# A GpSimd scaling step issued three steps later in an attention pipeline

## The chip, the cores and the metric

The kernel runs on one core of one Trainium2 chip. The metric is device time in microseconds (us), from launch to end. The kernel before takes 1523.18 us, the median of three runs (1522.98 to 1523.98).

## The reference

Four layers stand one behind the other, each with a residual: a spectral filter, an attention, and the same two again with the same weights. The sequence has 2048 rows of 512 values in bfloat16.

```python
x = x + A(layernorm(x))      # A: rfft2, times (w_r + 1j*w_i), irfft2
x = x + B(layernorm(x))      # B: attention, 32 query heads of width 16, one key/value head
x = x + A(layernorm(x))
x = x + B(layernorm(x))

scores = einsum("bhqd,bkd->bhqk", q, k) * 16 ** -0.5
o = einsum("bhqk,bkd->bhqd", softmax(scores), v)
B = o.transpose(0, 2, 1, 3).reshape(1, 2048, 512) @ wo
```

Only the attention matters here. Its softmax is divided late: the kernel carries one extra column of ones beside v, which gives the sum of the weights, and each head's output is multiplied by the reciprocal of that sum.

## The kernel before, in words

Each of the two attention layers is cut into 32 **groups**, numbered from 0: four query blocks of 512 rows, and in each eight groups of four heads. A group has 64 score tiles of 128 keys by 512 queries, 16 key chunks for each of four heads. `run` (L560) writes out one order for all engines by hand. It goes in **steps**: 579 for a layer, 18 for a group (the first group has 20). A step n does this:

- `act_step` (L780): TensorE makes three or two score tiles in turn (`sc`, L681), and ScalarE takes the exponential of all of them in one instruction (`e`, L790).
- `dv_score` and `dv_pass` (L809, L819): TensorE makes one more score tile (`dv`, L681). VectorE turns it into a first image (`t_new`, L824), an integer whose bits, read as bfloat16, approximate the exponential. Nineteen tiles of a group (thirteen of the first) go this way, in batches of six, seven and six. The score banks for `dv` are two, used by turns. A projection (below) borrows one of them from the step that issues it to the next.
- `image_step` (L827): each batch needs three more images, which differ from the first by an added constant. VectorE makes two of them, each for the whole batch in one **image pass** (`s_new`, L839), at the first and the fourth of the batch's six steps. GpSimd makes the third, tile by tile (`pool_new`, L843), over the same six steps: two tiles in the first step of the seven-tile batch and one in each later one. `pace` (L685) makes each of these GpSimd instructions wait for the image pass issued last.
- `pv_step` (L792): TensorE multiplies images and exponentials, two or more steps old, with the values (`pv_new`, L803).

Counted from a group's first step, the seven-tile batch has steps 6 to 11 and the third batch steps 12 to 17. So the image passes of the seven-tile batch are issued in steps 6 and 9, and the third batch's in steps 12 and 15. This text calls them **pass 6, pass 9, pass 12 and pass 15**, after their steps.

When a group's sum is complete, in step 3 of the next group, `evict` (L696) lets VectorE transpose it out of PSUM (L706), one step later take the reciprocal of the sums (L707), and three steps later GpSimd multiply the values with it: `normalise` (L734). For query blocks 0 to 2 that is one instruction (L739) which writes into `block`. After a block's eighth group, `turned_block` (L726) has the SyncE queue turn the block with four DMA transposes (L732) for the output projection. In query block 3 the multiplication is L717, and after every second group VectorE transposes the result back (L723), again three steps later.

Two kinds of projection are placed among the steps. The next group's queries (L485) come in step 7 of every group, with a VectorE instruction each in the next two steps (L491, L495). The output projection of a finished block (L754) comes in step 13 of groups 9 to 12, 17 to 20 and 25 to 28, with the residual on VectorE (L759) a step later. In step 13 of these groups no `pv_new` is issued.

All instructions of an engine keep the order in which they are issued. The functions `later` and `later_pool` put a call into a step that lies so many steps ahead. In a step, the calls of `later` come before the images, and those of `later_pool` behind the images and before `pv_step`.

Of the kernel before, what the change touches and what calls it, by code (L numbers as in the profile page):

```python
# [18 lines left out]
NT, NC, R, T, NQB, HG = 16, 4, 4, 4, 4, 8  # L19
# [453 lines left out]
class Attention:  # L473
# [86 lines left out]
    def run(self, row_done, work, psums, final):  # L560
# [25 lines left out]
        NG = NQB * HG  # L586
# [35 lines left out]
        for n0 in range(NS):  # L622
            lst = []
            if n0 in d_phase:
                g, b, k, tiles = d_phase[n0]
# [29 lines left out]
        for n in range(NS + LAG + 2):  # L655
# [5 lines left out]
            g = evict_at.get(n + 1)  # L661
# [23 lines left out]
        def pace(ins):  # L685
            if image[0] is not None:
                tc.add_manual_dep(ins.ins, image[0].ins.name, mybir.DependencyInfo(
                    mybir.DependencyClass.Sync, mybir.DependencyReason.DATA), reason="pace")

        def later(steps, fn):  # L690
            todo.setdefault(now[0] + steps, []).append(fn)

        def later_pool(steps, fn):
            todo_pool.setdefault(now[0] + steps, []).append(fn)

        def evict(g):  # L696

            ps = pv.pop(g)
            o = small.tile([P, 16, 32], F32, tag="oraw")
            den = small.tile([P, 16], F32, tag="den")  # L700
            if g == NG - 1:
                for half in HALVES:
                    nc.vector.transpose(out=o[:, half, :].rearrange("p c j -> p (c j)"), in_=ps[:, 32 * half.start:32 * half.stop])
                ends.extend((o, den))
                return
            nc.vector.transpose(out=o.rearrange("p c j -> p (c j)"), in_=ps)  # L706
            later(1, lambda: nc.vector.reciprocal(out=den, in_=o[:, :, DH]))  # L707
            later_pool(3, lambda: normalise(g, o, den))

        ends = []  # L710

        def scaled_values(engine, g, o, den, c=slice(0, 16)):
            if g % 2 == 0:
                od_new = small.tile([P, 16, 32], BF, tag="od")
                turned_od[g // 2] = od_new
            half = slice(DH * (g % 2), DH * (g % 2) + DH)
            return engine.tensor_tensor(out=turned_od[g // 2][:, c, half], in0=o[:, c, 0:DH],  # L717
                                        in1=den[:, c].unsqueeze(2).broadcast_to([P, c.stop - c.start, DH]), op=ALU.mult)
# [3 lines left out]
        def turned_back(g, c=slice(0, 16)):  # L722
            nc.vector.transpose(out=otc[g // HG][:, g % HG // 2, 32 * c.start:32 * c.stop],  # L723
                                in_=turned_od[g // 2][:, c, :].rearrange("p c j -> p (c j)"))

        def turned_block(qb):  # L726

            turned = small.tile([P, 4, 512], BF, tag="be", bufs=1)
            otc[qb] = turned
            flat = od8[0].rearrange("p a b -> p (a b)")  # L730
            for h in range(4):
                nc.sync.dma_start(out=turned[:, h, :].rearrange("p (c q) -> p c q", c=16), in_=flat[32 * h:32 * h + 32, :], transpose=True)  # L732

        def normalise(g, o, den):  # L734
            if g < NG - HG:
                if g % HG == 0:
                    block = small.tile([P, 4, 512], BF, tag="bx", bufs=1)
                    od8[0] = block
                pace(nc.gpsimd.tensor_tensor(out=od8[0].rearrange("p a (c g d) -> p (a c) g d", c=4, g=HG)[:, :, g % HG, :], in0=o[:, :, 0:DH],  # L739
                                             in1=den.unsqueeze(2).broadcast_to([P, 16, DH]), op=ALU.mult))  # L740
                if g % HG == HG - 1:
                    turned_block(g // HG)
                return
            if g % HG == 0:
                ot_new = small.tile([P, 4, 512], BF, tag="otc", bufs=2)
                otc[g // HG] = ot_new
            pace(scaled_values(nc.gpsimd, g, o, den))
            if g % 2:
                later(3, lambda: turned_back(g))
# [115 lines left out]
        for n in range(NS + LAG + 2):  # L865
            now[0] = n
            act_step(n)
            dv = dv_score(n)
            for fn in pending:
                fn()  # L870
            del pending[:]
            if n in evict_at:
                evict(evict_at[n])
            dv_pass(n, dv)
            for fn in todo.pop(n, ()):
                fn()
            image_step(n)
            for fn in todo_pool.pop(n, ()):
                fn()
            pv_step(n)  # L880
            if n in piece_at:
                piece(*piece_at[n])
            for i, k in EARLY.get(NS - n, ()) if final else ():
                if k == 0:
                    ps = psd.tile([P, 512], F32, tag=f"dv{i}")
                    early.append(ps)
                last_project(i, early[i], (k,))
            chain()
# [260 lines left out]
```

## Time and profile before

| what | value |
|---|---|
| median of three runs | 1523.18 us |
| the profiled execution's own time | 1522.62 us |
| its span, first to last instruction | 1520.8 us |
| mean granted TensorE clock | 0.994 |
| busy: TensorE, VectorE, ScalarE, GpSimd | 88%, 93%, 94%, 51% |

The profile's page gives each engine's busy time and the costliest groups of instructions. The timeline view lists one engine's instructions in order of time: start in us, duration in us, engine, line, operation, what is written and read, its shape, and how many of one kind follow each other (x3). In square brackets stands the idle time before it and what ended that. Of several instructions in one row the duration covers them all, and records of one engine may overlap a little, since the next starts while the last one drains. The windows view adds up each engine's busy time in a stretch.

### The profile page before, as it was taken

The numbers are of one execution on the slowest core, as the hardware profiler recorded it, in microseconds if no ns is written. First come the engines' busy times: TensorE is split into PE (matmuls) and PEld (weight loads), VectorE is DVE, ScalarE is ACT, GpSimd is POOL, SyncE is SP. The second block draws the span as 40 slices with busy tenths as digits, with TensorE's granted clock in tenths as the row PEclk, the third lists the DMA queues.
The fourth block names the chain that finished last, engine by engine and source line by source line (L and its number), as shares of the span: only waits on it lengthen the run. The fifth ranks groups of instructions, "written<-read, shape, count | busy, mean of one in ns | idle before, by whom it ended". The sixth has DMA issues, their size and how long they took to land.

```text
span 1520.8 us, 33089 instructions
## 1 busy us (share of the span) xinstructions
PE 1337.1 (88%) x13186; PEld 427.5 (28%) x13186; DVE 1421.6 (93%) x2267; ACT 1427.3 (94%) x1349; POOL 780.1 (51%) x1310
## 2 busy tenths in 40 slices
PE   5988888899889988999899788889998899889987
PEld 2532222222222222222235222222222222222222
DVE  7888999999999999999989899999999999999996
ACT  4669999999999999999965899999999999999998
POOL 1005555555566555655600155555656555665555
PEclk9999999999999999999999899999999999999999
DMA  8120000100000000100010200000000000010000
GB/s 291 22 56 2 2 1 2 15 2 1 2 16 2 1 1 2 15 2 1 2 47 14 43 1 2 2 1 19 5 2 4 19 5 5 4 19 5 5 5 18
DMA packets 40655, 25.15 MB, mean 17 GB/s; under 512 B 31796, under 2 KB 37940, under 8 KB 40244
## 3 DMA queue, kind: packets, MB, share of 16 engines
q1 hardware_dynamic: 40116, 21.99, 5.8%
q8 instruction: 103, 1.69, 0.5%
q0 software_dynamic: 384, 1.05, 0.2%
q14 instruction: 52, 0.43, 0.1%
HBM read 14.64 MB, written 2.10 MB: 11 GB/s over the span
## 4 chain that ended last, share of the span: by engine, by line
ACT 51%; issue 22%; DVE 15%; PE 7%; POOL 1%; POOLq 0%; DVEq 0%; ACTq 0%
ACT e L790 49%; DVE t_new L824 7%; DVE s_new L839 4%; PE sc L681 1%; PE pv_new L803 1%; DVE st L161 1%; PE new L273 1%; PE new L443 1%; POOL pool_new L843 1%; DVE o L706 1%; PE new L311 0%; PE new L413 0%; DVE x_sb L459 0%; PE dv L681 0%; ACT X_new L188 0%
## 5 line engine op out<-in xcount | busy, mean ns | idle before, releaser
L790 ACT ACTIVATE e<-sc 128x1536 bf16<-128x1536 f32 (+1 forms) x1158 | 1312.7, 1300 | 4.2 <-PE dv L681 2.6
L843 POOL TENSOR_SCALAR pool_new<-t_new 128x512 int16<-128x512 int16 x1204 | 729.5, 629 | 701.9 <-DVE s_new L839 609.3
L824 DVE TENSOR_SCALAR t_new<-dv 128x512 uint16<-128x512 f32 x1204 | 790.1, 678 | 61.7 <-PE dv L681 54.3
L803 PE MATMUL pv_new<-e,vaug 128*32 128x512 bf16 x2892 | 583.3, 386 | 0.0
L681 PE MATMUL sc<-qt,KT 32*128 32x512 bf16 x2892 | 455.1, 384 | 123.4 <-ACT e L790 118.6
L681 PE MATMUL dv<-qt,KT 32*128 32x512 bf16 x1204 | 450.6, 384 | 18.9 <-DVE t_new L824 16.0
L803 PE MATMUL pv_new<-s_new,vaug 128*32 128x512 bf16 x2408 | 426.6, 385 | 1.9 <-DVE s_new L839 1.2
L839 DVE TENSOR_SCALAR s_new<-t_new 128x3584 int16<-128x3584 int16 (+1 forms) x380 | 403.3, 1062 | 0.1
L681 PEld LDWEIGHTS <-KT 32*128 32x128 bf16 x4096 | 157.9, 91 | 563.0 <-issue 559.7
L803 PE MATMUL pv_new<-pool_new,vaug 128*32 128x512 bf16 x1204 | 300.9, 384 | 1.4 <-POOL pool_new L843 1.4
L803 PEld LDWEIGHTS <-vaug 128*32 128x32 bf16 x7708 | 155.2, 94 | 370.4 <-issue 339.0
L803 PE MATMUL pv_new<-t_new,vaug 128*32 128x512 bf16 x1204 | 231.3, 385 | 0.1
L485 PE MATMUL ps<-xz,wq_sb 128*128 128x512 bf16 x248 | 65.2, 385 | 0.9 <-DVE t_new L824 0.8
L273 PE MATMUL new<-tab_F,xz 128*128 128x512 bf16 x192 | 46.5, 389 | 7.4 <-DVE xz L237 7.4
L491 DVE TENSOR_SCALAR qt<-ps,kq 128x512 bf16<-128x512 f32 x62 | 46.0, 742 | 1.2 <-PE ps L485 1.2
L706 DVE STREAM_TRANSPOSE o<-pv_new 128x512 f32<-128x512 f32 x62 | 43.7, 706 | 0.0
L188 ACT ACTIVATE X_new<-x_sb,ln_nb,ln_rstd 128x512 bf16<-128x512 bf16 x43 | 32.8, 804 | 8.0 <-DVE ln_nb L173 5.6
L161 DVE BATCH_NORM_STATS2 st<-x_sb 128x6 f32<-128x512 bf16 x52 | 33.5, 676 | 3.9 <-DMA x_sb<-in_A_x_dram 3.7
L168 ACT ACTIVATE ln_rstd<-ln_mv,ln_eps 128x4 f32<-128x4 f32 (+1 forms) x15 | 4.5, 297 | 30.8 <-DVE ln_mv L165 30.8
L485 PEld LDWEIGHTS <-wq_sb 128*128 128x128 bf16 x256 | 22.1, 97 | 32.2 <-issue 17.1
L739 POOL TENSOR_TENSOR block<-o,den 128x256 bf16<-128x256 f32 x48 | 29.9, 623 | 0.0
L197 ACT CAST x_new<-new 128x1024 bf16<-128x1024 f32 x14 | 14.2, 1012 | 16.4 <-PE new L311 15.1
(125 smaller groups left out, 586.0 us busy)
## 6 DMA issues: line engine op xcount, KB each, us to landing
tab_F<-const_F SPq DMA_DIRECT2D x5, 640.0 KB, 8.6
t_new<-const_IE SPq DMA_DIRECT2D x2, 1024.0 KB
x_sb<-in_A_x_dram SPq DMA_DIRECT2D x3, 512.0 KB, 7.0
rt<-in_A_w_r_dram SPq DMA_DIRECT2D x1, 1028.0 KB, 8.4
rt<-in_A_w_i_dram SPq DMA_DIRECT2D x1, 1028.0 KB, 6.6
t_new<-const_IO SPq DMA_DIRECT2D x2, 512.0 KB
woh<-in_B_wo_dram SPq DMA_DIRECT2D x16, 64.0 KB, 2.4
out_dram<-x_sb SPq DMA_DIRECT2D x8, 128.0 KB, 2.4
```

The lines of the kernel that those rows point to most:

```text
L161: self.nc.vector.bn_stats(st, x_t[:, r, :])
L188: engine.activation(out=xn_ap, in_=x_ap, func=ACT.Identity, bias=nb, scale=rs)
L273: self.mm(ps, lhsT=z, rhs=tab, start=start and i == 0, stop=stop and i == len(mms) - 1)
L485: self.nc.tensor.matmul(ps, lhsT=self.aw["wq"][:, c, hg, :], rhs=self.xT[:, 4 * qb:4 * qb + 4, c, :], start=(c == 0), stop=(c == NC - 1))
L491: self.nc.vector.tensor_scalar(out=qt, in0=ps, scalar1=self.kq[:, 1:2], scalar2=None, op0=ALU.mult)
L681: nc.tensor.matmul(dst, lhsT=KT[hs, kc * P:(kc + 1) * P], rhs=QT[g][hs, :], start=True, stop=True)
L706: nc.vector.transpose(out=o.rearrange("p c j -> p (c j)"), in_=ps)
L790: nc.scalar.activation(out=e[:, 0:na, :], in_=sc[:, 0:na, :], func=ACT.Exp, scale=SCALE)
L803: nc.tensor.matmul(pv[g][32 * h:32 * h + 32, :], lhsT=vaug[:, max(j, 0), kc, :], rhs=rhs, start=(first_pv[(g, h)] == u), stop=(last_pv[(g, ...
L824: nc.vector.tensor_scalar(out=tb[(g, b)][:, i, :], in0=dv, scalar1=T_MUL, scalar2=T_ADD, op0=ALU.mult, op1=ALU.add)
L839: image[0] = nc.vector.tensor_scalar(out=s_new[:, lo:nt, :], in0=src[:, lo:nt, :], scalar1=PH_OFF[i], scalar2=None, op0=ALU.add)
L843: pace(nc.gpsimd.tensor_scalar(out=sb[(g, b, 3)][:, i, :], in0=src[:, i, :], scalar1=1.0, scalar2=PH_OFF[3], op0=ALU.mult, op1=ALU.add))
```

## The change

One number in `evict` is replaced. For query blocks 0 to 2 (`g` below 24) the multiplication is issued six steps behind the eviction, and no longer three. Query block 3 keeps three.

```diff
             nc.vector.transpose(out=o.rearrange("p c j -> p (c j)"), in_=ps)
             later(1, lambda: nc.vector.reciprocal(out=den, in_=o[:, :, DH]))
-            later_pool(3, lambda: normalise(g, o, den))
+            later_pool(3 if g >= NG - HG else 6, lambda: normalise(g, o, den))
```

The eviction lies in step 3 of the next group. So the instruction L739 moves from step 6 to step 9 of groups 1 to 24 of each layer, 48 instances. On GpSimd's queue it stood behind the seven-tile batch's first two tiles and ahead of its third and fourth. It now stands behind the fifth tile, which is the first one after pass 9, and ahead of the sixth and seventh. Through `pace` it waits for pass 9 where it waited for pass 6. After groups 7, 15 and 23 the four DMA transposes move along with it. Nothing else changes: the number of instructions, their shapes and the work of the other engines stay.

## The prediction

> **What bounds the kernel now.** I began with the page's costliest groups, to see which engine is full and how much time each party to the change takes.
>
> ```profile
> L790 ACT ACTIVATE e<-sc 128x1536 bf16<-128x1536 f32 (+1 forms) x1158 | 1312.7, 1300 | 4.2 <-PE dv L681 2.6
> L843 POOL TENSOR_SCALAR pool_new<-t_new 128x512 int16<-128x512 int16 x1204 | 729.5, 629 | 701.9 <-DVE s_new L839 609.3
> L739 POOL TENSOR_TENSOR block<-o,den 128x256 bf16<-128x256 f32 x48 | 29.9, 623 | 0.0
> ```
>
> ScalarE's exponentials fill 1312.7 us and wait 4.2 us in all, so they set the end. The moved instruction lasts 0.623 us. GpSimd has 701.9 us of idle time, so its own total matters to nobody; what matters is whom it holds up. That needs the timeline of one group: first VectorE, then GpSimd, in group 9 of the first attention layer (pass 6 starts at 300.81, pass 9 at 304.54, pass 12 at 307.76).
>
> ```profile
> 300.81 1.08 DVE L839 TENSOR_SCALAR s_new<-t_new 128x3584 int16<-128x3584 int16 x1
> ...
> 304.54 1.48 DVE L839 TENSOR_SCALAR s_new<-t_new 128x3584 int16<-128x3584 int16 x1
> 305.95 1.90 DVE L824 TENSOR_SCALAR t_new<-dv 128x512 uint16<-128x512 f32 x3
> 307.76 0.95 DVE L839 TENSOR_SCALAR s_new<-t_new 128x3072 int16<-128x3072 int16 x1
> 308.63 0.68 DVE L824 TENSOR_SCALAR t_new<-dv 128x512 uint16<-128x512 f32 x1
> 309.23 0.68 DVE L759 TENSOR_TENSOR x_sb<-ps,x_sb 128x512 bf16<-128x512 f32 x1
> ```
>
> ```profile
> 302.08 1.21 POOL L843 TENSOR_SCALAR pool_new<-t_new 128x512 int16<-128x512 int16 x2 [1.37 <-PE ps L485]
> 303.25 0.62 POOL L739 TENSOR_TENSOR block<-o,den 128x256 bf16<-128x256 f32 x1
> 303.84 1.24 POOL L843 TENSOR_SCALAR pool_new<-t_new 128x512 int16<-128x512 int16 x2
> 306.11 1.79 POOL L843 TENSOR_SCALAR pool_new<-t_new 128x512 int16<-128x512 int16 x3 [1.03 <-DVE s_new L839]
> 308.89 1.79 POOL L843 TENSOR_SCALAR pool_new<-t_new 128x512 int16<-128x512 int16 x3 [0.99 <-DVE s_new L839]
> ```
>
> Pass 9 has the shape of pass 6 and takes 1.48 us where that takes 1.08. GpSimd's five instructions end at 303.84 + 1.24 = 305.08, 0.54 us after the pass has begun. The pass ends at 306.02, 0.94 behind them. Pass 12 too meets GpSimd, which ends at 306.11 + 1.79 = 307.90, but for 0.14 us only. It takes 0.95, as passes do that meet nothing, and ends at 308.71, 0.81 behind GpSimd. So here an image pass overlaps GpSimd's last 0.14 us for nothing, and waits for the rest. The figures are the same within 0.02 us in nearly every group.
>
> **Does ScalarE feel the 0.4 us?** A group lasts 20.37 us from pass 6 to pass 6, and 20.41 where an output projection stands in it. I took the ends of single exponentials in the trace: the median distance is 1.344 us to one of three tiles and 0.916 to one of two. Nine of each make 20.34. So a group loses 0.03 us, at the exponential of step 10, and one with an output projection 0.03 more, at step 16. The first loss comes before pass 9's wait: that exponential starts at 304.98, and what holds its scores up is the `dv` of step 8, which waits for the image tile behind pass 6. Pass 9's wait costs ScalarE nothing.
>
> **The change, part by part.**
>
> *Behind pass 6.* GpSimd has four instructions in place of five. They end 0.58 us earlier (303.84 − 303.25 = 0.59), at 304.50, ahead of pass 9. Pass 9 then takes its free time. The nearest row is 1.04 us, for the same pass in group 26 of the second layer (below), where a VectorE instruction stands ahead of it and GpSimd is done. It ends at 305.58, 0.44 earlier.
>
> *Behind pass 9.* GpSimd starts 0.09 behind the pass (306.11 − 306.02), at 305.67, with four instructions in place of three. At 0.585 us from start to start the last one starts at 307.43 and ends at 308.05: 0.15 later than the 307.90 of now. Pass 12 is ready earlier than before, but no earlier than 307.6: the third `t_new` ahead of it needs the `dv` of step 12, and TensorE makes that only once the exponential of step 10 has ended, at 306.43. By step 6's rows, where nothing else delays it, a pass starts 1.15 us behind the start of its step's scores. They start at 306.48, so the pass at 307.63. GpSimd's last instruction runs by then, and pass 12 ends at 308.05 + 0.81 = **308.86, 0.15 later**, and lasts 1.23. The collision isn't gone. It has moved from pass 9 to pass 12, with 0.42 us of overlap for 0.54, in a place where GpSimd was already at the limit.
>
> *Who waits for pass 12.* The group with a transposition (L723) ahead of pass 9 shows it, in rows of before. In groups 25 and 26 of the second layer, both with an output projection:
>
> ```profile
> 1375.33 1.08 DVE L839 TENSOR_SCALAR s_new<-t_new 128x3584 int16<-128x3584 int16 x1
> ...
> 1382.28 0.95 DVE L839 TENSOR_SCALAR s_new<-t_new 128x3072 int16<-128x3072 int16 x1
> ...
> 1395.74 1.08 DVE L839 TENSOR_SCALAR s_new<-t_new 128x3584 int16<-128x3584 int16 x1
> ...
> 1400.09 1.04 DVE L839 TENSOR_SCALAR s_new<-t_new 128x3584 int16<-128x3584 int16 x1
> 1401.06 1.87 DVE L824 TENSOR_SCALAR t_new<-dv 128x512 uint16<-128x512 f32 x3
> 1402.86 0.96 DVE L839 TENSOR_SCALAR s_new<-t_new 128x3072 int16<-128x3072 int16 x1
> ...
> 1416.33 1.08 DVE L839 TENSOR_SCALAR s_new<-t_new 128x3584 int16<-128x3584 int16 x1
> ```
>
> Pass 12 ends 7.90 us behind pass 6 in group 25 and 8.08 in group 26, 0.18 later. The groups last 20.41 and 20.59: the 0.18 is lost in full. The path is in TensorE's timeline of group 9.
>
> ```profile
> 308.85 0.39 PE L681 MATMUL sc<-qt,KT 32*128 32x512 bf16 x3
> 309.36 0.37 PE L681 MATMUL dv<-qt,KT 32*128 32x512 bf16 x1
> ```
>
> The output projection holds the other bank, so the `dv` of step 14 needs the bank that the first `t_new` behind pass 12 (308.63 + 0.68 = 309.31) empties. It starts 0.05 us behind that, and everything behind it on TensorE shifts, up to the scores for step 16, where ScalarE already loses 0.03. Group 30 of the second layer has the same transposition, no output projection, and pass 12 at 8.08 (1477.79 to 1484.91 + 0.96). It lasts 20.38: there the delay is hidden, behind 0.73 us in which VectorE waits for TensorE at the group's end.
>
> *The sum.* Of the 24 groups of a layer that receive the instruction, 9 to 12 and 17 to 20 have an output projection: 8, and 16 in both layers. 16 × 0.15 = 2.4 us. In the other 32 the cost is taken as 0. Their cover is thin in two places: GpSimd's three instructions behind pass 12 then end 0.11 into pass 15 (free up to 0.14), and TensorE needs the seven-tile batch's last GpSimd tile 0.15 later, in step 13, where it now idles 0.28 before the next scores. If both failed, the 32 would pay up to 0.15 each, 4.8 more.
>
> *The rest.* Behind L739 on GpSimd wait the sixth and seventh tile of the image, counted above. The buffers `o` and `den` are two each, and are next written two groups later. The four DMA transposes are issued 3 steps later (3.4 us). They take some 6 us to issue and 2.8 to land; their reader, the first output projection, comes 22 steps (25 us) later, and SyncE's queue has nothing behind them for 150 us. I cost these at nothing.
>
> *A rule against the trace.* Pass 9 met 0.54 us of GpSimd and lost 0.40 to 0.44; pass 12 met 0.14 and lost 0.01. The Trainium skill (SBUF — State Buffer, "Who interferes with whom") says that the two share one port pair under an exclusive lock, so that whoever comes second waits for the first's whole instruction. By that rule alone the moved instruction finds the next pass wherever it stands, and the trace agrees. It disagrees by 0.14 us on where the wait begins.
>
> **The sum against the times.** The profiled execution took 1522.62 us, its span 1520.8; with 2.4 more that is 1525.0. It lies 0.56 under the median of 1523.18. I predict for the median: **1525.6 us**, 0.16% slower. A measurement of this kernel can tell about 0.2% (3 us) from no change.
>
> **The rivals.**
>
> *The delay is hidden everywhere.* Pass 12's 0.15 us would have to vanish in the 16 groups too. The 0.44 us gained at pass 9 speaks for it, since TensorE's image products of step 11 run earlier; groups 26 and 28 of both layers, which all lose 0.18, speak against. It gives 1523.2.
>
> *VectorE was the bound.* Then 48 × 0.44 = 21 us would go, to 1502. VectorE is 93% busy, but ScalarE is full in every group, and all that it loses in these groups is 48 × 0.03 + 16 × 0.03 = 1.9 us. At best that is 1521.3.
>
> *A full block.* If a waiting pass had to do its whole 0.95 us behind GpSimd, pass 12 would end at 309.00, 0.29 later, and the 16 groups cost 4.6: 1527.8. Pass 9's 0.94 behind GpSimd, for 1.04 alone, speaks against. This is what the skill's lock (same section) makes if read to the letter.
>
> *Slower: pass 12 wins the race.* If it is ready before GpSimd's last instruction starts at 307.43, it goes ahead of it, and the batch's last tile ends near 308.95, 1.05 later than now. TensorE waits for that tile in step 13 of the 32 groups without an output projection. Of the 1.05 it has 0.28 idle, and the exponential of step 14 stands 0.23 behind its scores (15.90 − 15.18 − 0.49, in us of the group), so some 0.5 us are lost in each: 16 us, 1540. It decides at 0.2 us from my 307.63.
>
> *The instruction doesn't land there.* The step count gives the place without doubt; I give this nothing.
>
> **How the numbers follow.** Forecast 0.67; hidden everywhere 0.13; full block 0.06; the 32 groups paying as well (1530.4) 0.04; the race 0.04; a gain 0.04; 0.02 for what I don't see. The forecast's own range is 1524 to 1527, from 0.10 to 0.20 us per group and half a microsecond between runs. With the hidden case and the full block: 1522.9 to 1528.0. Over 1526.2 (0.2%) lie the last cases on that side, 0.14, and an eighth of the forecast, 0.09. Faster 0.04, same 0.73, slower 0.23.
>
> **What would show it.** Pass 9 at 1.04 to 1.08 us, pass 12 at about 1.23 in groups 1 to 24, unchanged in 25 to 31; groups 9 to 12 and 17 to 20 at 20.55, the others at 20.37. Wrong would be pass 12 at 0.95, groups without an output projection over 20.40, or GpSimd's fourth instruction behind pass 12.

## The result and the profile after

The changed kernel takes 1525.93 us, the median of 14 runs, beside 1523.11 for the kernel before in as many. The ratio is 1.0017, with a 95% interval of 1.0010 to 1.0024: some 2.6 us slower, and at least 1.5.

The two profiled executions differ by more, 1526.65 for 1522.62 us. But 1.4 us of that lie in the loading ahead of the first attention groups and in group 0 of the second attention layer, where the change has no part. So I also compare the lengths of single groups, from pass 6 of one to pass 6 of the next. Groups that a run leaves as they were agree within 0.03 us between executions, most within 0.01, but for single stalls.

Group 9 of the first layer after the change, VectorE's timeline first (start, duration, instruction), with the lines that answer to those of before:

```profile
301.61 1.08 DVE L839 TENSOR_SCALAR s_new<-t_new 128x3584 int16<-128x3584 int16 x1
...
305.33 1.08 DVE L839 TENSOR_SCALAR s_new<-t_new 128x3584 int16<-128x3584 int16 x1
...
307.82 0.69 DVE L824 TENSOR_SCALAR t_new<-dv 128x512 uint16<-128x512 f32 x1 [0.21 <-PE dv L681]
308.43 1.25 DVE L839 TENSOR_SCALAR s_new<-t_new 128x3072 int16<-128x3072 int16 x1
309.60 0.67 DVE L824 TENSOR_SCALAR t_new<-dv 128x512 uint16<-128x512 f32 x1
...
322.19 1.08 DVE L839 TENSOR_SCALAR s_new<-t_new 128x3584 int16<-128x3584 int16 x1
```

Pass 9 now takes 1.08 us for 1.48, and pass 12 takes 1.25 for 0.95. Ahead of pass 12 VectorE even waits 0.21 us for TensorE, so most of the time saved at pass 9 could not be used. GpSimd's timeline shows what pass 12 meets.

```profile
302.88 2.41 POOL L843 TENSOR_SCALAR pool_new<-t_new 128x512 int16<-128x512 int16 x4 [1.37 <-PE ps L485]
306.50 0.62 POOL L843 TENSOR_SCALAR pool_new<-t_new 128x512 int16<-128x512 int16 x1 [1.21 <-DVE s_new L839]
307.08 0.62 POOL L739 TENSOR_TENSOR block<-o,den 128x256 bf16<-128x256 f32 x1
307.67 1.20 POOL L843 TENSOR_SCALAR pool_new<-t_new 128x512 int16<-128x512 int16 x2
```

The four instructions behind pass 9 end at 307.67 + 1.20 = 308.87, 0.44 us after pass 12 has begun. The pass ends at 309.68, 0.81 behind them. Counted from pass 6 that is 8.07 us, where it was 7.90 before: 0.17 later. TensorE's timeline shows who pays:

```profile
309.54 0.40 PE L681 MATMUL sc<-qt,KT 32*128 32x512 bf16 x3
310.33 0.37 PE L681 MATMUL dv<-qt,KT 32*128 32x512 bf16 x1 [0.40 <-DVE t_new L824]
```

The `dv` of step 14 waits for the image tile behind pass 12 (309.60 + 0.67 = 310.27) and starts 8.72 us behind pass 6, for 8.55. The group lasts 322.19 − 301.61 = 20.58 us, for 20.41. So it goes in 15 of the 16 groups with an output projection that received the instruction: they lose 0.15 to 0.17 us each. In the other one, group 20 of the second layer, pass 12 comes late in both kernels, here at 7.18 us, and takes its free 0.95. Of the 32 groups without a projection 30 are as long as before within 0.02 us, 20.38 for 20.37 in most. The other two are groups 16 and 24 of the first layer. They lose 0.16 and 0.15; the first experiment comes back to them.

### The profile page after: what moved, and what is told of

Read it like the earlier page. It is cut to its first block, busy times and chain, and to the rows that moved or that the text cites. A ratio compares the mean times of both kernels' runs of the same rounds, so it can differ in the third digit from the quotient of the medians.

```text
span 1524.9 us, 33048 instructions
## 1 busy us (share of the span) xinstructions
PE 1332.3 (87%) x13145; PEld 428.9 (28%) x13186; DVE 1418.2 (93%) x2267; ACT 1429.0 (94%) x1349; POOL 780.1 (51%) x1310
## 3 DMA queue, kind: packets, MB, share of 16 engines
q0 software_dynamic: 384, 1.05, 0.2%
## 4 chain that ended last, share of the span: by engine, by line
ACT 47%; issue 20%; DVE 16%; PE 10%; POOL 1%; DVEq 0%; POOLq 0%; ACTq 0%
ACT e L790 46%; DVE t_new L824 7%; DVE s_new L839 4%; PE pv_new L803 3%; PE sc L681 2%; DVE st L161 1%; PE dv L681 1%; PE new L273 1%; PE new L443 1%; POOL pool_new L843 1%; DVE o L706 1%; DVE x_sb L459 0%; PE new L311 0%; PE new L413 0%; PE new L375 0%
## 5 line engine op out<-in xcount | busy, mean ns | idle before, releaser
L803 PE MATMUL pv_new<-e,vaug 128*32 128x512 bf16 x2892 | 591.1, 387 | 0.0
L803 PE MATMUL pv_new<-s_new,vaug 128*32 128x512 bf16 x2408 | 417.9, 385 | 1.2 <-DVE s_new L839 1.2
L839 DVE TENSOR_SCALAR s_new<-t_new 128x3584 int16<-128x3584 int16 (+1 forms) x380 | 397.3, 1046 | 0.1
L803 PE MATMUL pv_new<-pool_new,vaug 128*32 128x512 bf16 x1204 | 297.8, 385 | 1.4 <-POOL pool_new L843 1.3
L739 POOL TENSOR_TENSOR block<-o,den 128x256 bf16<-128x256 f32 x48 | 29.7, 619 | 0.0
```

The lines of the kernel that those rows point to most:

```text
L803: nc.tensor.matmul(pv[g][32 * h:32 * h + 32, :], lhsT=vaug[:, max(j, 0), kc, :], rhs=rhs, start=(first_pv[(g, h)] == u), stop=(last_pv[(g, ...
L839: image[0] = nc.vector.tensor_scalar(out=s_new[:, lo:nt, :], in0=src[:, lo:nt, :], scalar1=PH_OFF[i], scalar2=None, op0=ALU.add)
```

## The experiments

Two measures stand for each run: the ratio of its time to the kernel before, with the 95% interval, and from the profiled executions how much longer than before all groups of a kind last together, in us. Single stalls of a group, which come and go between executions, shift such a sum by up to 0.4. Where the second column shows +0.31 to +0.41, groups 16 and 24 of the first layer make up 0.31 to 0.33 of it.

| run | ratio | 16 groups with a projection | 32 without | groups 25 to 30, both layers |
|---|---|---|---|---|
| the change | 1.0017 (1.0010 to 1.0024) | +2.34 | +0.40 | −0.05 |
| e1_rest | 0.9999 (0.9990 to 1.0008) | −0.09 | +0.31 | −0.07 |
| e2_proj | 1.0020 (1.0011 to 1.0029) | +2.36 | −0.03 | −0.06 |
| e3_two_later | 1.0017 (1.0009 to 1.0026) | +2.44 | +0.32 | −0.08 |
| e4_step15 | 0.9997 (0.9988 to 1.0006) | −0.70 | +0.02 | −0.06 |
| e5_step12 | 0.9997 (0.9988 to 1.0006) | −0.63 | +0.04 | −0.06 |
| e6_twice_rest | 1.0198 (1.0178 to 1.0217) | +2.35 | +29.07 | −0.04 |
| e7_proj15 | 0.9992 (0.9983 to 1.0001) | −0.64 | +0.41 | −0.93 |
| e8_proj15_before | 0.9994 (0.9985 to 1.0003) | −0.50 | +0.04 | −0.92 |
| e9_both15 | 0.9996 (0.9987 to 1.0004) | −0.61 | +0.09 | −0.92 |
| e10_twice_behind | 1.0021 (1.0012 to 1.0030) | +2.47 | +0.40 | −0.05 |

### One half of the groups at a time

```diff
-            later_pool(3 if g >= NG - HG else 6, lambda: normalise(g, o, den))
+            later_pool(3 if g >= NG - HG or (g > 7 and g % 8 < 4) else 6, lambda: normalise(g, o, den))   # e1_rest
+            later_pool(6 if 7 < g < NG - HG and g % 8 < 4 else 3, lambda: normalise(g, o, den))           # e2_proj
```

> The multiplication moves only in the 32 groups without an output projection; the 16 with one keep it in step 6. If the cost sits where the output projection stands behind pass 12, these 32 groups last 20.38 us as in the changed kernel (20.37 before), and the time is within 0.5 us of the kernel before. If each of the 48 moved instructions costs the same part of the 2.8 us, it is 1.9 us slower. If VectorE's saved wait at pass 9 is worth something, it is faster.

> The opposite: the multiplication moves only in the 16 groups with an output projection (9 to 12 and 17 to 20 of both layers). By the theory the whole cost is here: these groups last 20.57 us for 20.41, and the time is 2.6 us above the kernel before. If the cost is spread evenly over the moved instructions, it is 0.9 us above.

The two halves come apart cleanly. Moved in the 32 groups alone, the time is that of before (1522.63 for 1523.37 us). Moved in the 16 alone, it is 1526.64, as slow as the whole change. In both runs pass 9 takes 1.08 to 1.09 and pass 12 1.25 to 1.26 us in the groups where the instruction moved, but for one in each, where pass 12 comes too late to wait. So pass 12's delay arises nearly everywhere. It costs where the projection stands behind it, and in two groups more. An even share for each moved instruction is out.

The two are groups 16 and 24 of the first layer, with +0.31 us together in e1_rest. Pass 15 of group 16 and the pass in step 0 of the next group read before:

```profile
454.32 0.95 DVE L839 TENSOR_SCALAR s_new<-t_new 128x3072 int16<-128x3072 int16 x1
...
458.11 1.26 DVE L839 TENSOR_SCALAR s_new<-t_new 128x3072 int16<-128x3072 int16 x1
```

And in the changed kernel, where pass 6 of this group starts 1.47 us later (445.39 for 443.92):

```profile
455.96 0.95 DVE L839 TENSOR_SCALAR s_new<-t_new 128x3072 int16<-128x3072 int16 x1
...
459.59 1.41 DVE L839 TENSOR_SCALAR s_new<-t_new 128x3072 int16<-128x3072 int16 x1
```

Two layer-norm instructions on VectorE (L152, L153) stand between passes 12 and 15 here and hand the delay on to pass 15, 0.17 us. GpSimd's tiles behind pass 15 shift with it, and in these two groups four small layer-norm instructions (L179 to L182) lie among them. So the next pass meets GpSimd for longer: 1.41 us for 1.26, and the group loses as much. In groups 13 to 15 and 21 to 23 of the same layer the two VectorE instructions are there and the four on GpSimd are not, and nothing is lost. I read this from the rows; no run moved the four.

### The pass or the late tiles

```diff
-            later_pool(3 if g >= NG - HG else 6, lambda: normalise(g, o, den))
+            later_pool(3 if g >= NG - HG else 8, lambda: normalise(g, o, den))
```

> The multiplication two steps later still, in step 11: behind the seven-tile batch's last tile and not ahead of its sixth, but still between pass 9 and pass 12. GpSimd then ends as late as in the changed kernel, while its image tiles come as early as before or earlier. If pass 12 waiting for GpSimd is the cause, pass 12 again lasts 1.25 us and the time is 2.5 to 3 us above the kernel before. If the late image tiles are the cause, the time is that of the kernel before.

Here GpSimd makes all three tiles first. Its timeline in group 5 of the first layer, and VectorE's pass 12:

```profile
225.79 1.78 POOL L843 TENSOR_SCALAR pool_new<-t_new 128x512 int16<-128x512 int16 x3 [1.21 <-DVE s_new L839]
227.53 0.62 POOL L739 TENSOR_TENSOR block<-o,den 128x256 bf16<-128x256 f32 x1
```

```profile
227.72 1.25 DVE L839 TENSOR_SCALAR s_new<-t_new 128x3072 int16<-128x3072 int16 x1
```

The last two tiles are 0.58 us earlier than in the changed kernel, the multiplication ends as late as the last tile did there (228.15, 0.43 into the pass), and the cost is the same: +2.44 us in the 16 groups. The pass is the cause, not the tiles.

### Behind pass 15, and behind pass 12

```diff
-            later_pool(3 if g >= NG - HG else 6, lambda: normalise(g, o, den))
+            later_pool(3 if g >= NG - HG else 12, lambda: normalise(g, o, den))   # e4_step15
+            later_pool(3 if g >= NG - HG else 9, lambda: normalise(g, o, den))    # e5_step12
```

> The multiplication in step 15, behind pass 15, where GpSimd is done 1.4 us (with an output projection 0.9 us) before the next group's first pass. It then meets no pass. Pass 9 takes 1.04 to 1.08 us, pass 12 0.95 with its end 0.13 us earlier than before, pass 15 and the next group's first pass are as before. By the theory ScalarE gets back at most the 0.03 us at step 16 of the 16 groups with an output projection: 20.38 for 20.41, 0.5 us below the kernel before. If VectorE were the bound, the 0.44 us of 48 groups would be gained: some 20 us.

> The multiplication in step 12, behind pass 12. Passes 9 and 12 then run free, and pass 12 ends 0.13 us earlier than before. GpSimd has four instructions between pass 12 and pass 15, so in groups 1 to 8 of the first layer and in most groups without an output projection of the second pass 15 meets its last 0.4 us and takes 1.2. Theory: that wait is hidden, as waits of 0.4 us at pass 15 are in single groups of before, and the time is 0 to 0.6 us below the kernel before. If every met pass costs its wait, the groups with a longer pass 15 lose 0.27 us each, and the time is 5 us or so above.

With the multiplication behind pass 15, group 9's passes 6, 9 and 12 and the next group's pass 6 read:

```profile
300.49 1.08 DVE L839 TENSOR_SCALAR s_new<-t_new 128x3584 int16<-128x3584 int16 x1
304.20 1.09 DVE L839 TENSOR_SCALAR s_new<-t_new 128x3584 int16<-128x3584 int16 x1
307.30 0.95 DVE L839 TENSOR_SCALAR s_new<-t_new 128x3072 int16<-128x3072 int16 x1
...
320.86 1.08 DVE L839 TENSOR_SCALAR s_new<-t_new 128x3584 int16<-128x3584 int16 x1
```

None of them waits, VectorE has its 0.4 us back in all 48 groups, and the group lasts 20.37 us for 20.41. The 16 groups give 0.70 us together, 0.03 to 0.05 each but for one with a stall, and the ratio's interval holds 1. A bound VectorE would have shown 20 us. With the multiplication behind pass 12 (e5_step12), pass 15 takes 1.22 us in groups 1 to 8, and they last 20.38: a wait of 0.27 us on VectorE that nobody feels.

### The projection moved out of the way

```diff
-ROUNDS, QSTEP, OSTEP, STAT, HOLD, QABS = (2, 4), 7, 13, 14, 8, 1
+ROUNDS, QSTEP, OSTEP, STAT, HOLD, QABS = (2, 4), 7, 15, 14, 8, 1
```

This edit alone, with the multiplication in step 6, is e8_proj15_before; added to the change it is e7_proj15.

> The changed kernel with the output projections in step 15 instead of 13, so that no borrowed score bank waits for the image tile behind pass 12. Theory: pass 12 still lasts 1.25 us, but nothing is lost by it; the time is within 0.6 us of the same layout with the multiplication in step 6 (the next kernel). If pass 12's delay costs by itself, it stays 2.6 us above that.

> The kernel before with the output projections in step 15 instead of 13: the partner of the kernel above. The borrowed bank now waits for the image tile of step 15, which lies ahead of pass 15. The groups with an output projection should last 20.37 to 20.45 us, and the time is within 1.5 us of the kernel before.

In e7_proj15, group 9 of the first layer reads on VectorE:

```profile
301.88 1.08 DVE L839 TENSOR_SCALAR s_new<-t_new 128x3584 int16<-128x3584 int16 x1
...
308.70 1.25 DVE L839 TENSOR_SCALAR s_new<-t_new 128x3072 int16<-128x3072 int16 x1
...
322.26 1.08 DVE L839 TENSOR_SCALAR s_new<-t_new 128x3584 int16<-128x3584 int16 x1
```

Pass 12 is delayed just as in the changed kernel, and the group lasts 20.38. The two kernels take 1522.84 and 1522.92 us. So with the projection elsewhere the change costs 0.2 us: by the table 0.37 more in the 32 groups, 0.34 of it in groups 16 and 24 of the first layer, and 0.14 less in the 16. That shows that the projection in step 13 is needed for the loss. Groups 26 of both layers and 28 of the second, which lost 0.17 to 0.18 to a transposition ahead of pass 9, last 20.38 too. They make up 0.63 of the 0.93.

The run moves all of the projection at once: the borrowed bank, the work on TensorE and the residual on VectorE (L759). That the bank is what counts follows from two rows more. In the changed kernel the `dv` of step 14 waits 0.40 us for `t_new` and starts 8.72 us behind pass 6; here it starts at 7.94 and waits for nothing. And the residual's 0.68 us on VectorE is not enough by itself: the layer-norm instructions of groups 13 to 15 and 21 to 23 in the first layer take 0.68 and 0.18, stand between the same two passes and hand the delay on to pass 15, and in the changed kernel these groups last 20.38 us for 20.37.

### The multiplication doubled

```diff
+            if g < NG - HG and not (g > 7 and g % 8 < 4):
+                later_pool(6, lambda: again(o, den))    # e6_twice_rest; 8, also for normalise, in e10_twice_behind
+
+        spare = small.tile([P, 16, DH], BF, tag="spare", bufs=1)
+
+        def again(o, den):
+            pace(nc.gpsimd.tensor_tensor(out=spare, in0=o[:, :, 0:DH], in1=den.unsqueeze(2).broadcast_to([P, 16, DH]), op=ALU.mult))
```

> The changed kernel with the multiplication done a second time, into a spare buffer, in the 32 groups without an output projection. It is work beyond the reference's. GpSimd then ends another 0.59 us later behind pass 9, 0.76 later than before, and with it the seven-tile batch's last tile and pass 12. The forecast put the cover of these groups at 0.28 us of TensorE's idle time and 0.23 us by which the exponential of step 14 stands behind its scores, 0.51 in all. By that the groups lose 0.2 to 0.3 us each: 20.6 to 20.7 us for 20.38, and the time is 9 to 12 us above the kernel before. If these groups hide any delay of this size, it is 2.8 above like the changed kernel.

This expectation failed: 1.0198, 30 us and not 9 to 12. Most of the 32 groups last 21.10 us, six of them another 1 us. The added lines shift the line numbers behind them by 7. GpSimd's last two tiles of the seven-tile batch in group 5 of the first layer, one by one:

```profile
229.15 0.61 POOL L850 TENSOR_SCALAR pool_new<-t_new 128x512 int16<-128x512 int16 x1
229.73 1.31 POOL L850 TENSOR_SCALAR pool_new<-t_new 128x512 int16<-128x512 int16 x1
```

VectorE's pass 12 and TensorE's image product in the same stretch:

```profile
229.33 1.24 DVE L846 TENSOR_SCALAR s_new<-t_new 128x3072 int16<-128x3072 int16 x1
```

```profile
231.10 0.38 PE L810 MATMUL pv_new<-pool_new,vaug 128*32 128x512 bf16 x1 [1.28 <-POOL pool_new L850]
```

Pass 12 was ready at 229.33, before GpSimd's last tile could start at 229.73. It waited for the tile under way only, then went first, and the last tile took 1.31 us and ended at 231.04. TensorE waited 1.28 us for it. This is the forecast's rival of the lost race, priced there at 0.5 us a group for a tile 1.05 us late. Here the tile ends 8.53 us behind pass 6, for 7.09 before, so 1.44 late, and it costs 0.73. The forecast's cover of 0.51 us would have left 0.93, so it was too small by 0.2. What the six longer groups lose on top I didn't follow up.

> The doubled multiplication again, as work beyond the reference's, in the 32 groups without an output projection, but both copies in step 11, behind the seven-tile batch's last tile. GpSimd has as much to do between pass 9 and pass 12 as in the run with the copies in step 9. If that run lost its 0.73 us a group because pass 12 went ahead of the last image tile and TensorE waited for that tile, the loss is gone here: the copy is what pass 12 overtakes, the groups last 20.38 us and the time is 2.5 to 3 us above the kernel before, as with one multiplication in step 11. If GpSimd's extra 0.6 us is the cause, the groups last 21.1 us again and the time is 25 to 30 us above.

The last run separates the late tile from GpSimd's added time. Both copies stand behind the last tile, and pass 12 overtakes the second copy:

```profile
229.80 0.62 POOL L746 TENSOR_TENSOR block<-o,den 128x256 bf16<-128x256 f32 x1
230.38 1.33 POOL L715 TENSOR_TENSOR spare<-o,den 128x256 bf16<-128x256 f32 x1
```

```profile
229.99 1.25 DVE L846 TENSOR_SCALAR s_new<-t_new 128x3072 int16<-128x3072 int16 x1
```

The copy is held up for 0.7 us, nobody needs it, and the 32 groups are as long as in the changed kernel, 20.38 us in most. The 0.73 us were the late tile's.

### Both free places together

This run takes the multiplication to step 15 and the output projections to step 15.

> Both moves that cost nothing by themselves: the multiplication in step 15, behind pass 15, and the output projections in step 15. Theory: passes 9, 12 and 15 wait for nothing and no group pays for a projection, also not 26 and 28: all groups at 20.38 us but for the few with single stalls, 16 x 0.03 + 8 x 0.03 + 4 x 0.17 = 1.4 us below the kernel before. Rival: the two moves meet in step 15 and 16, where VectorE then has the residual while GpSimd has four instructions, and some of it comes back: 0 to 1 us above the kernel before.

Most groups last 20.38 us, with a projection or without, and the three columns add up to −1.44 us, as forecast. That it comes so near is partly chance: single stalls in three of the 16 groups make up 0.18 of it. In the time it doesn't show: 1522.56 for 1523.75 us, 0.9996 with an interval that holds 1. None of the versions is shown to be faster than the kernel before.

## Why the prediction was right, point by point

*The place of the collision.* It was said to move from pass 9 to pass 12, and it did. Counted from pass 6, pass 12 was forecast to be ready at 6.82 us and GpSimd to end at 7.24; they came at 6.82 and 7.26. Pass 12 lasts 1.25 us (forecast 1.23) and ends 0.17 later (0.15).

*Pass 9's free time* was mis-sized: 1.08 us for 1.04. I had taken it from a pass that stands behind a transposition (L723) on VectorE. Behind a `t_new`, as here, a pass of this shape takes 1.08 whether GpSimd has ended 0.04, 0.10 or 0.9 us before; pass 6 of the very group showed it. That shifts GpSimd behind it and makes up the difference at pass 12.

*Nothing to gain at pass 9.* e4_step15 shows it: with the waits of passes 9 and 12 gone, the groups are as long as before, or 0.03 to 0.05 us shorter.

*Who pays.* Of the 16 groups with an output projection 15 pay the delay one for one, 0.15 to 0.17 us each, 2.45 in all; in the 16th a stall is 0.11 shorter, which makes 2.34. For the other 32 I took 0, and named two places where their cover is thin. Neither gave way: pass 15 then overlaps GpSimd's last 0.12 us and still takes 0.95 in most groups, and 30 groups pay 0.09 us together. But groups 16 and 24 of the first layer pay 0.31, by a third place, the layer-norm instructions, that the forecast had not looked at. So 2.4 us stands against 2.7 in the profiled groups and 2.6 by the ratio. That 2.34 alone comes so near to 2.4 is chance. e2_proj and e7_proj15 show that it is mainly the groups with a projection, and the rows of the `dv` that it is the borrowed bank in them.

*The rivals.* Hidden everywhere: out by e2_proj. VectorE as the bound: out by e4_step15. The 32 groups paying as well: out for 30 of them, true of two. A full block, which would end pass 12 0.95 us behind GpSimd: it ends 0.81 to 0.82 behind in 47 groups; in the 48th it starts too late to wait. The race was won by 0.18 us (GpSimd's last tile starts at 308.25, the pass at 308.43), where I had 0.20; e6_twice_rest shows what losing it costs. My expectation for that run forgot this rival, though it stood in the forecast.

*The lock.* The Trainium skill (SBUF — State Buffer, "Who interferes with whom") has the later of the two wait for the whole instruction of the earlier. The runs agree in both directions: pass 12 waits for one tile, and in e6_twice_rest the next tile waits for the pass. Only the last 0.14 us of a GpSimd record cost a pass next to nothing. The forecast also drew from the rule that the moved instruction finds the next pass wherever it stands. That is too strong: behind pass 15 it finds none (e4_step15).

## What to carry to other kernels

Taking an instruction out of one gap between two engines' collisions puts it into the next gap, which may have room (behind pass 15) or none (behind pass 9). So measure both gaps and count, behind the one that receives it, who waits for its end. A stall on a busy engine is worth nothing while another engine never idles, and the same stall costs in full where a borrowed buffer hangs on it. When an effect is 0.2%, the lengths of a kernel's repeating groups, taken from one profiled execution, tell more than the whole time does. Look at each of them: here the sum over 32 groups, divided by 32, hid two groups that paid and 30 that did not.

## What the hardware showed that I had not expected

A waiting VectorE pass goes ahead of GpSimd instructions that are already queued: it waits for the one under way, and the next one then takes 1.31 us for 0.62 (e6_twice_rest) or 1.33 (e10_twice_behind). So a queue of short GpSimd instructions delays a pass by at most one of them, in every image pass of all twelve profiles, and it is the queue that pays. And the free time of a pass of 128x3584 differs with the VectorE instruction ahead of it: 1.08 to 1.09 us behind a `t_new`, 1.04 to 1.05 behind a transposition.
